# Three edits of order and place in a pair of linear-attention blocks: PSUM banks of the second block's kv products, SBUF places of the raw x^T, order of the first transfers

## The chip, the cores and the metric

The kernel runs on one core of a Trainium2 chip. Time is device microseconds (us) of one execution. The kernel before takes 582.83 us (median of 3 runs, 582.18 to 585.84). Lower is better.

## The reference

Two independent blocks, A and B, have the same form; their outputs stand side by side in the last axis. With S = 2048 tokens, D = 640, H = 32 heads of 20:

```
qkv = x @ wqkv                       # q, k, v: [H, S, 20]
pq, pk = phi(q), phi(k)              # phi(t) = where(t > 0, t + 1, exp(t)) + 1e-6
kv  = einsum("hsd,hse->hde", pk, v)
z   = sum over s of pk
o   = (pq @ kv) / (pq . z + 1e-6)
out = o (heads joined) @ wo          # [S, 640] per block
```

## The kernel before

**What is computed in which form.** Every fp32 product that needs accuracy is made of three TensorE products: each operand is split into a high part (ScalarE, a copy that rounds) and a low part (VectorE, the raw value minus the high part), and high times high, high times low and low times high are summed in PSUM. kv is not formed from v: the kernel first sums G = x^T phi(k) over all tokens ("gacc", five row blocks of 128), then kv = wv^T G by groups of heads, masks it to its diagonal blocks, and multiplies it by wo. So after the k stage of a block there is one matrix M = kv wo (640 x 640) with which phi(q), divided, is multiplied. Products with wk and with M are in part done by a seven-product scheme on half blocks, with sums of operands made on VectorE.

**Two ways of setting order.** The k stage of both blocks is written as jobs (`note`, line 86) that a planner (`emit`, line 113) puts in order by due times with a model of each engine; TensorE's own order is that in which the jobs were written. A job's due time is worked back from those that need its result; among the jobs that can start, the one due first goes first. The same planner gives raw data their SBUF places: `BD` (line 256) has 7 places of 640 columns with the tag "wst", `BO` 4 and `GD` 31. The q stage behind it (from line 863 on) is written out by hand: `at(slot, f, ...)` hangs a step on a slot such as ("q", u, c, k), and `run` does what hangs there when the TensorE instructions of that slot have been written. u counts blocks of 512 tokens (u = 0 to 3 are block A's, 4 to 7 block B's), c the five column blocks of q, k the five parts of the contraction.

**The first transfers.** x^T of the first three token tiles ("xj", five row blocks) and wk (five row blocks, the first in two halves) come first: `load_joint` (line 626), the two halves at line 633 and `load` (line 286). xj's block 0 is issued by ScalarE's queue, all others by SyncE's (SP). TensorE has seven short products on a zero tile ("idle", line 614) ahead of the first real ones (`one`, line 661).

**The q stage's banks.** `bank` (line 865) hands out the eight PSUM banks in four rings (line 862): "one" is banks 0 to 2, "a" 3 and 4, "e" 5 and 6, "small" 7. `qmm` (line 1036) takes a bank of ring "one" for each of the five q products of a token block, 15 matmuls each; `qphi` then reads that bank twice on ScalarE (lines 1056 and 1057: exp and relu). In the first token block (u = 0), block B's kv products are put in between: `kvmm2` (line 941), for each of six groups of heads, two per q product in c = 0, 1, 2 (at k = 0 and k = 3). It also takes its bank ("pskv") from ring "one"; VectorE reads it once (line 952, the mask). `mmm2` (line 962) multiplies by wo in a bank of "a" and one of "e".

**The q stage's SBUF places.** Block B's wv, cut in six groups, is loaded by the planner into six of the seven "wst" places, group by group, and each is freed by the last matmul of its `kvmm2`. In the same slots the raw x^T of token block 1 ("xqs", five parts, `load_xraw`, line 916) is loaded into "wst" places too: `stage` (line 902) and `turned` (line 870) go round the seven places, 0 to 6. In the kernel before the planner has put group 0 of wv in place 0, group 5 in place 1, groups 1, 2, 3 and 4 in places 2, 3, 4 and 5; place 6 is free. Behind these loads SP's queue has, in written order, the first parts of block A's M forms ("fh", "fl", `form_load`, line 1018) and the low parts of x^T ("xql", `load_xq`, line 921). The low parts have six places: five hold token block 0's, so only the first of token block 1's can be loaded early, and each of the other four waits until TensorE has read one of block 0's for the last time, in ("q", 0, 4, k).

**Transfers in flight.** SP's transfers count on eight semaphores in turn ("DMAHW0" to "DMAHW7"): each waits until the one eight before it has landed. SP issues in order, so a transfer that waits holds up all behind it.

Of the kernel before, what the change touches and what calls it, by code (L numbers as in the profile page):

```python
# [75 lines left out]
class Plan:  # L76
# [6 lines left out]
        self.jobs = []  # L83
        self.pe_at = 0.0

    def note(self, engine, n, fn, w, r, ahead=None, dma=None, late=None, by=None):
        base = self.RATE.get(engine)
        j = Job(engine, base[0] + base[1] * n if base else n, fn, ahead, dma)
        for part, writes in [(p, True) for p in w] + [(p, False) for p in r]:
            sp = part.space  # L90
            if sp.where is not None and sp not in j.spaces:
                j.spaces.append(sp)
            for lo, hi, other, wrote in sp.uses:
                if lo < part.hi and part.lo < hi and (writes or wrote) and other is not j:
                    j.deps.add(other)
            if writes:
                sp.uses = [u for u in sp.uses if not (part.lo <= u[0] and u[1] <= part.hi and u[2] is not j)]
            sp.uses.append((part.lo, part.hi, j, writes))
        for d in j.deps:
            d.nexts.append(j)  # L100
        for sp in j.spaces:
            sp.left += 1
        if engine == "PE":
            j.ideal = self.pe_at
            self.pe_at += j.cost
        j.late = self.pe_at + (25.0 if late is None else late)
        if by is not None:
            j.late = self.pe_at + by
        j.by = by
        self.jobs.append(j)  # L110
        return j

    def emit(self, start, log=None):
        jobs = self.jobs
        for j in reversed(jobs):
            due = min([n.due - LAG for n in j.nexts], default=j.late)
            if j.by is not None:
                due = min(due, j.late)
            due -= j.cost + (2.2 + j.dma if j.dma else 0)
            if j.engine == "PE":  # L120
                due = min(due, j.ideal)
            j.due = due

        def take(sp):
            for s in sp.where:
# [10 lines left out]
        n = 0  # L136
# [67 lines left out]
def tile_linear_attn_pair(ctx: ExitStack, tc: tile.TileContext, ins, out: bass.AP):  # L204
    nc = tc.nc
    P = 128
    S, D = ins[0]["x"].shape
# [3 lines left out]
    HF = D // 2  # L211
# [54 lines left out]
    note = plan.note  # L266
# [16 lines left out]

    BK = [Bank("bank", k) for k in range(8)]

    def load(dst, src, n, ahead=14.0, eng=None):
        eng = eng or nc.sync
        note("SP", 0.07, lambda: eng.dma_start(dst.f, src), [dst], [], ahead=ahead, dma=n * 512 / 330e3)

    def hi_of(hi, src, n):  # L290
        note("ACT", n, lambda: act(hi.r, src.f, AF.Copy), [hi], [src], ahead=10.0)
# [332 lines left out]
    jr, wr = [Space("xj", 3 * P, ANY) for _ in range(NC)], [Space("wk", D, ANY) for _ in range(NC)]  # L624

    def load_joint(c, eng):
        src = ins[0]["xt"][c * P:(c + 1) * P, 0:3 * P]
        note("SP", 0.07, lambda: eng.dma_start(jr[c].all.f, src), [jr[c].all], [], dma=0.6)

    load_joint(0, nc.scalar)  # L630
    for h in range(2):
        cs = slice(h * HF, (h + 1) * HF)
        note("SP", 0.07, lambda h=h, cs=cs: nc.sync.dma_start(wr[0][h * HF:h * HF + HF].f, ins[0]["wk"][:P, cs]),
             [wr[0][h * HF:h * HF + HF]], [], dma=0.5)
    for c in range(1, NC):
        load_joint(c, nc.sync)
        load(wr[c].all, ins[0]["wk"][c * P:(c + 1) * P, :], D, None)

    def whalf(h, *t):
        return [x[0][h * HF:h * HF + HF] for x in t]  # L640
# [124 lines left out]
    for p in range(4, NPB):  # L765
        i, h = divmod(p - 2, 2)
# [9 lines left out]
    for p in range(NPB + 2, NP):  # L776
        i, h = divmod(p - NPB - 2, 2)
# [17 lines left out]
    j = note("HOST", 0.0, swap, [gate.all], [])  # L795
# [9 lines left out]
    wst, whl, wvt, xt, xts = {}, {}, {}, {}, {}  # L805
# [41 lines left out]
    for g, (h0, nh) in enumerate(GROUPS):  # L847
        cols = NC * DH * nh
        w = Space("wv", cols, (BD,))
# [5 lines left out]
        whl[k] = hi.tile, lo.tile  # L855
    for k, (hi, lo) in list(xt.items()):
        xt[k] = [hi.tile, lo.tile]
    for k, w in list(wvt.items()):
        wvt[k] = w.all.f.rearrange("p (c e) -> p c e", c=NC)
    close_pool(kg, "kg")  # L860
# [2 lines left out]
    pn, turn = {}, {}  # L863

    def bank(name, tag="one", bufs=3):
        at, n = ptags[tag]
        pn[tag] = pn.get(tag, -1) + 1
        return psum.tile([P, 512], F32, name=name, tag=f"bank{at + pn[tag] % n}", bufs=1)

    def turned(tag, n):  # L870
        turn[tag] = (turn.get(tag, -1) + 1) % n
        return f"{tag}{turn[tag]}"

    lows = []

# [26 lines left out]
    def stage(name):  # L902
        return base.tile([P, D], F32, name=name, tag=turned("wst", 7), bufs=1)
# [37 lines left out]
    def kvmm2(b, g):  # L941
        h0, nh = GROUPS[g]
        r = DH * nh
        w = wvt.pop((b, g))
        ps = bank("pskv")
        for c in range(NC):
            gd = gacc[b, c].rearrange("p (d h) -> p d h", h=H)[:, :, h0:h0 + nh]
            nc.tensor.matmul(ps[:r, :r].rearrange("p (d h) -> p d h", h=nh), w[:, c, :], gd,  # L948
                             start=(c == 0), stop=(c == NC - 1))
        t = base.tile([r, r], F32, name="kvt", tag="kvt0", bufs=1)  # L950
        hi, lo = (base.tile([r, r], F32R, name=f"kv{t}", tag=turned("kvs", 12), bufs=1) for t in "hl")
        nc.vector.tensor_tensor(t, ps[:r, :r], mask[nh][:r, :], op=OP.mult)
        split(hi, lo, t)
        kvt[b, g] = (hi, lo)
# [299 lines left out]
    h = NG - 1  # L1254
# [24 lines left out]
    for v in range(1, NU):  # L1279
        w, u = v - 1, v + 1  # L1280
# [86 lines left out]
```

## Time and profile before

| | |
|---|---|
| median of 3 runs | 582.83 us (582.18 to 585.84) |
| the profiled execution's own time | 583.46 us |
| its span in the profile | 581.6 us |
| TensorE busy | 568.3 us, 98% of the span |
| VectorE, ScalarE busy | 431.0 us (74%), 341.8 us (59%) |
| granted TensorE clock, mean | 0.996 |

The span is shared out between engines in the profile's first part. The timeline gives each instruction's start, its length and, in brackets, how long its engine had been idle before it and what ended that. The waits list adds up those times by pair of instructions. A name such as `psq<-xqh,wh` is the output and the operands by the program's names. "SPq" rows are the issue of a transfer, not the transfer. The windows view gives, for a stretch of time, each engine's busy time with the count of instructions in brackets, the granted clock ("PEclk"), and the share of time that the transfer engines were busy.

### The profile page before, as it was taken

What the parts mean: (1) busy time and instruction counts of PE and PEld (TensorE: products, weight loads), DVE (VectorE), ACT (ScalarE), POOL (GpSimd) and SP (SyncE); (2) the same over time, 40 slices, a digit from 0 to 9 for tenths busy, and PEclk for the clock granted to TensorE, in tenths of its full rate; (3) what the DMA queues carried; (4) which work ended last, traced back from release to release, by engine and by line L of the source; (5) the groups of instructions that cost most, each with busy time, mean ns of one, the idle gap of its engine ahead of it and who ended that gap; (6) DMA issues with size and microseconds to landing.
All of it is one profiled execution on the core that took longest, in us unless ns stands there. A gap on an engine that the chain in (4) does not pass through costs nothing.

```text
span 581.6 us, 9507 instructions
## 1 busy us (share of the span) xinstructions
PE 568.3 (98%) x3541; PEld 537.7 (92%) x3541; DVE 431.0 (74%) x700; ACT 341.8 (59%) x619; POOL 57.3 (10%) x93
## 2 busy tenths in 40 slices
PE   8999999999999999999989799999999999999997
PEld 6999999999998999999967689898998989898897
DVE  7688687689777878874444498967789775757792
ACT  6878465573769766763435565744647455545541
POOL 0210011110011011111000001211011200001010
PEclk9999999999999999999999899999999999999999
DMA  8994847748768898778745975674183897122022
GB/s 311 368 249 121 218 115 191 195 115 265 240 160 254 280 279 250 202 211 249 238 109 190 391 263 171 223 248 157 63 278 109 310 393 258 70 74 92 0 91 90
DMA packets 67857, 117.60 MB, mean 202 GB/s; under 512 B 6500, under 2 KB 29668, under 8 KB 67812
## 3 DMA queue, kind: packets, MB, share of 16 engines
q1 hardware_dynamic: 59060, 89.94, 47.3%
q0 software_dynamic: 8608, 26.88, 16.7%
q8 instruction: 27, 0.44, 0.3%
q10 hardware_dynamic: 144, 0.20, 0.1%
q14 instruction: 18, 0.15, 0.1%
HBM read 71.11 MB, written 35.39 MB: 183 GB/s over the span
## 4 chain that ended last, share of the span: by engine, by line
PE 89%; DMA 5%; issue 2%; ACT 2%; DVE 1%; SPq 0%; ACTq 0%; DVEq 0%; POOLq 0%
PE psg L300 23%; PE pa L1167 12%; PE ka L300 8%; PE psq L888 8%; PE psq L889 8%; PE psq L890 7%; PE pe L1167 6%; PE ke L300 4%; PE psk L689 4%; PE psb L1167 4%; PE kb L300 3%; DMA zacc<-ek 2%; DMA xql<-xd 1%; DMA xqs<-in_A_xt 1%; PE pskv L948 1%
## 5 line engine op out<-in xcount | busy, mean ns | idle before, releaser
L300 PE MATMUL psg<-pkh,xnh 128*128 128x320 f32 x320 | 99.1, 310 | 0.0
L300 PE MATMUL psg<-pkl,xnh 128*128 128x320 f32 x320 | 98.8, 309 | 0.0
L300 PE MATMUL psg<-pkh,xnl 128*128 128x320 f32 x320 | 98.7, 308 | 0.0
L888 PE MATMUL psq<-xqh,wh 128*128 128x512 f32 x200 | 79.4, 397 | 3.7 <-ACT rq L1057 3.7
L889 PE MATMUL psq<-xql,wh 128*128 128x512 f32 x200 | 78.7, 394 | 3.1 <-DMA xql<-xd 3.1
L890 PE MATMUL psq<-xqh,wl 128*128 128x512 f32 x200 | 78.6, 393 | 0.0
L300 PEld LDWEIGHTS psg<-pkh,xnh 128*128 128x128 f32 x320 | 60.0, 188 | 0.1
L300 PEld LDWEIGHTS psg<-pkl,xnh 128*128 128x128 f32 x320 | 60.1, 188 | 0.0
L300 PEld LDWEIGHTS psg<-pkh,xnl 128*128 128x128 f32 x320 | 60.1, 188 | 0.0
L1182 ACT ACTIVATE o<-pa 128x320 f32<-128x320 f32 x64 | 28.0, 438 | 47.1 <-PE pa L1167 46.9
L1058 DVE SCALAR_TENSOR_TENSOR pq<-eq,rq 128x512 f32<-128x512 f32 x40 | 27.6, 690 | 35.5 <-ACT rq L1057 35.5
L471 ACT ACTIVATE kt<-ka 128x320 f32<-128x320 f32 x52 | 22.7, 437 | 52.9 <-PE ka L300 52.3
L388 POOL DMA_DIRECT2D zacc<-ek x32 | 26.4, 836 | 244.5 <-DVE ek L481 186.7
L519 DVE TENSOR_TENSOR gacc<-psg,gacc 128x320 f32<-128x320 f32 x60 | 29.1, 489 | 28.1 <-PE psg L300 27.3
L888 PEld LDWEIGHTS psq<-xqh,wh 128*128 128x128 f32 x200 | 37.8, 189 | 12.2 <-ACT rq L1057 5.0
L889 PEld LDWEIGHTS psq<-xql,wh 128*128 128x128 f32 x200 | 38.0, 190 | 10.8 <-DMA xql<-xd 3.5
L1056 ACT ACTIVATE eq<-psq 128x512 f32<-128x512 f32 x40 | 24.0, 599 | 40.6 <-PE psq L890 38.2
L890 PEld LDWEIGHTS psq<-xqh,wl 128*128 128x128 f32 x200 | 38.0, 190 | 8.1
L383 ACT ACTIVATE pkh<-ek,epst 128x640 fp32r<-128x640 f32 x32 | 26.5, 829 | 8.5 <-DVE ek L481 8.4
L1167 PE MATMUL pa<-fh,dah 128*128 128x320 f32 x96 | 29.7, 309 | 0.0
L1167 PE MATMUL pa<-fl,dah 128*128 128x320 f32 x96 | 29.6, 309 | 0.0
L1167 PE MATMUL pa<-fh,dal 128*128 128x320 f32 x96 | 29.6, 308 | 0.0
(212 smaller groups left out, 1551.7 us busy)
## 6 DMA issues: line engine op xcount, KB each, us to landing
zacc<-ek POOLq DMA_DIRECT2D x32, 320.0 KB, 5.0
xql<-xd SPq DMA_DIRECT2D x40, 256.0 KB, 5.3
xd<-xl SPq DMA_DIRECT2D x29, 320.0 KB, 4.5
out<-o POOLq DMA_DIRECT2D x28, 320.0 KB, 3.6
xns<-in_A_x SPq DMA_DIRECT2D x16, 320.0 KB, 4.2
xts<-in_B_xt_tiles SPq DMA_DIRECT2D x16, 320.0 KB, 4.2
xns<-in_B_x SPq DMA_DIRECT2D x16, 320.0 KB, 6.8
xqs<-in_A_xt SPq DMA_DIRECT2D x20, 256.0 KB, 4.8
```

Of the source, the lines that this page charges most:

```text
L300: nc.tensor.matmul(o, a.r, w.r, start=start and k == i == 0, stop=k == n - 1 and i == 2, skip_group_check=True)
L383: note("ACT", n + 110, lambda: act(hi.r, p.f, AF.Identity, bias=epst), [hi], [p, K0.all], by=8.0)
L388: note("POOL", 1.0, lambda: nc.gpsimd.dma_start(z.f, p.f, **kw), [z], [p], dma=1.0 if first else 1.86)
L519: tt(o, BK[k].tile[:, :HF], o, op=OP.add)
L689: nc.tensor.matmul(o[h][:, :HF], x[a].r, w[c][h * HF:h * HF + HF].r, start=c == 0 and i == 0, stop=c == NC - 1 and i == 2, skip_group_chec ...
L888: nc.tensor.matmul(o, whi, xhi, start=first, stop=False)
L889: nc.tensor.matmul(o, whi, xlo, start=False, stop=False)
L890: nc.tensor.matmul(o, wlo, xhi, start=False, stop=last)
L1056: nc.scalar.activation(e, ps, AF.Exp)
L1058: nc.vector.scalar_tensor_tensor(pq[u][:, c, :], e, 1.0, r, op0=OP.min, op1=OP.add)
L1167: nc.tensor.matmul(ps, x, y, start=start and n == i == 0, stop=n == len(terms) - 1 and i == 2, skip_group_check=True)
L1182: copy = lambda x, y: nc.scalar.activation(x, y, AF.Copy)
```

## The change

It has three parts.

- `kvmm2` takes its bank from ring "e" (banks 5 and 6) in place of ring "one" (banks 0 to 2).
- The ring of "wst" places starts with those that hold no group of wv, and then goes through the groups' places in the order of the groups. In the changed kernel the planner puts group 0 in place 6 and leaves place 0 free; the others stand as before. The ring is then 0, 6, 2, 3, 4, 5, 1, so the five parts of xqs of token block 1 go to the free place and to the places of groups 0, 1, 2 and 3. Before, they went to places 0, 1, 2, 3, 4: those of groups 0, 5, 1, 2 and 3.
- The first transfers have due times that are set by hand: wk's first half, xj's block 0, wk's second half, and then xj and wk of block 1, 2, 3, 4 in turn.

```diff
-    def note(self, engine, n, fn, w, r, ahead=None, dma=None, late=None, by=None):
+    def note(self, engine, n, fn, w, r, ahead=None, dma=None, late=None, by=None, due=None):
...
-        j.by = by
+        j.by, j.set = by, due
...
-            j.due = due
+            j.due = due if j.set is None else j.set
...
-    def load(dst, src, n, ahead=14.0, eng=None):
-        eng = eng or nc.sync
-        note("SP", 0.07, lambda: eng.dma_start(dst.f, src), [dst], [], ahead=ahead, dma=n * 512 / 330e3)
+    def load(dst, src, n, ahead=14.0, due=None):
+        note("SP", 0.07, lambda: nc.sync.dma_start(dst.f, src), [dst], [], ahead=ahead, dma=n * 512 / 330e3, due=due)
...
-        note("SP", 0.07, lambda: eng.dma_start(jr[c].all.f, src), [jr[c].all], [], dma=0.6)
-
-    load_joint(0, nc.scalar)
+        note("SP", 0.07, lambda: eng.dma_start(jr[c].all.f, src), [jr[c].all], [], dma=0.6, due=-99.0 + 2 * c)
     for h in range(2):
         cs = slice(h * HF, (h + 1) * HF)
         note("SP", 0.07, lambda h=h, cs=cs: nc.sync.dma_start(wr[0][h * HF:h * HF + HF].f, ins[0]["wk"][:P, cs]),
-             [wr[0][h * HF:h * HF + HF]], [], dma=0.5)
+             [wr[0][h * HF:h * HF + HF]], [], dma=0.5, due=-100.0 + 2 * h)
+    load_joint(0, nc.scalar)
     for c in range(1, NC):
         load_joint(c, nc.sync)
-        load(wr[c].all, ins[0]["wk"][c * P:(c + 1) * P, :], D, None)
+        load(wr[c].all, ins[0]["wk"][c * P:(c + 1) * P, :], D, None, -98.0 + 2 * c)
...
+    places = [w.slot[1] for w in wvt.values()]
+    places = [i for i in range(7) if i not in places] + places
...
-        return f"{tag}{turn[tag]}"
+        return f"{tag}{places[turn[tag]] if tag == 'wst' else turn[tag]}"
...
-        ps = bank("pskv")
+        ps = bank("pskv", "e", 2)
```

TensorE's instructions stand in the same order in both kernels; what differs there are waits. The first place is TensorE at the switch from block B's second kv group to the end of the first q product (u = 0, c = 0, k = 4) and on to c = 1: `psq` is a q product's bank, `pskv` a kv product's, and the brackets name the engines or transfers whose semaphores an instruction waits for. Before:

```order
L948 MATMUL pskv<-gacc,wv 120x120 [waits DMAHW0_49]
L948 MATMUL pskv<-gacc,wv 120x120 x4
L888 MATMUL psq<-xqh,wh 128x512 [waits Activation_49]
L889 MATMUL psq<-xql,wh 128x512 [waits DMAHW7_49]
L890 MATMUL psq<-xqh,wl 128x512 [waits DVE_49]
L888 MATMUL psq<-xqh,wh 128x512 [waits Activation_49]
L889 MATMUL psq<-xql,wh 128x512
```

Now:

```order
L948 MATMUL pskv<-gacc,wv 120x120 [waits DMAHW0_49,PE_49]
L948 MATMUL pskv<-gacc,wv 120x120 x4
L888 MATMUL psq<-xqh,wh 128x512 [waits Activation_49]
L889 MATMUL psq<-xql,wh 128x512 [waits DMAHW7_49]
L890 MATMUL psq<-xqh,wl 128x512 [waits DVE_49]
L888 MATMUL psq<-xqh,wh 128x512
L889 MATMUL psq<-xql,wh 128x512
```

The wait for ScalarE (Activation) at the first matmul of the q product c = 1 is gone, and so it is at c = 2 and c = 3; the kv product of group 1 now follows TensorE's own earlier use of its bank.

The second place is SP in the same stretch: the five raw parts of x^T (xqs), the first three pairs of M forms (fh, fl) and the first low parts (xql) of token block 1. The order of the transfers is the same; the waits differ. Before:

```order
L919 DMA xqs<-in_A_xt 128x512 [waits DMAHW2_49,PE_49]
L919 DMA xqs<-in_A_xt 128x512 [waits DMAHW3_49,PE_49]
L919 DMA xqs<-in_A_xt 128x512 [waits DMAHW4_49]
L919 DMA xqs<-in_A_xt 128x512 [waits DMAHW5_49]
L1032 DMA fh<-fdh_90 128x640 [waits DMAHW6_49]
L1032 DMA fl<-fdl_91 128x640 [waits DMAHW7_49]
L919 DMA xqs<-in_A_xt 128x512 [waits DMAHW0_49]
L1032 DMA fh<-fdh_92 128x640 [waits DMAHW1_49]
L1032 DMA fl<-fdl_93 128x640 [waits DMAHW2_49]
L1032 DMA fh<-fdh_94 128x640 [waits DMAHW3_49]
L1032 DMA fl<-fdl_95 128x640 [waits DMAHW4_49]
L923 DMA xql<-xd_81 128x512 [waits DMAHW5_49]
```

Now:

```order
L919 DMA xqs<-in_A_xt 128x512 [waits DMAHW2_49]
L919 DMA xqs<-in_A_xt 128x512 [waits DMAHW3_49,PE_49]
L919 DMA xqs<-in_A_xt 128x512 [waits DMAHW4_49,PE_49]
L919 DMA xqs<-in_A_xt 128x512 [waits DMAHW5_49,PE_49]
L1032 DMA fh<-fdh_90 128x640 [waits DMAHW6_49]
L1032 DMA fl<-fdl_91 128x640 [waits DMAHW7_49]
L919 DMA xqs<-in_A_xt 128x512 [waits DMAHW0_49,PE_49]
L1032 DMA fh<-fdh_92 128x640 [waits DMAHW1_49]
L1032 DMA fl<-fdl_93 128x640 [waits DMAHW2_49]
L1032 DMA fh<-fdh_94 128x640 [waits DMAHW3_49]
L1032 DMA fl<-fdl_95 128x640 [waits DMAHW4_49]
L923 DMA xql<-xd_81 128x512 [waits DMAHW5_49]
```

Before, the second xqs waited for TensorE's kv product of group 5, the last, and the third, fourth and fifth had nothing left to wait for there. Now each waits for one group in turn: none, 0, 1, 2, 3.

The third place is the start on VectorE, where the high and low parts of the first xj and wk are made (ScalarE makes the other high parts in the same new order: wk's first half ahead of xj's columns 128 to 383). Before:

```order
L648 CAST xjh<-xj 128x128
L294 TENSOR_TENSOR xjl<-xj,xjh 128x128
L294 TENSOR_TENSOR xjl<-xj,xjh 128x256
L294 TENSOR_TENSOR wkl<-wk,wkh 128x320
L294 TENSOR_TENSOR wkl<-wk,wkh 128x640
L294 TENSOR_TENSOR wkl<-wk,wkh 128x320
```

Now:

```order
L646 CAST xjh<-xj 128x128
L293 TENSOR_TENSOR xjl<-xj,xjh 128x128
L293 TENSOR_TENSOR wkl<-wk,wkh 128x320
L293 TENSOR_TENSOR xjl<-xj,xjh 128x256
L293 TENSOR_TENSOR wkl<-wk,wkh 128x320
L293 TENSOR_TENSOR xjl<-xj,xjh 128x384
```

wk's first half now goes ahead of xj's 256 columns, and wk's second half ahead of wk's block 1. Because the planner goes on from another state, some neighbours on ScalarE and VectorE change places later in the k stage too, above all while block A's kv and wo parts are made.

## The prediction

> **What bounds the kernel now.** I read the page's engine shares first, then the list of waits for TensorE (PE), then the timeline around each wait, then SP's timeline.
>
> ```profile
> PE 568.3 (98%) x3541; PEld 537.7 (92%) x3541; DVE 431.0 (74%) x700; ACT 341.8 (59%) x619; POOL 57.3 (10%) x93
> ...
> PE psq L888 <- ACT rq L1057: 3.7, 3, 1.2
> PE psq L889 <- DMA xql<-xd: 3.1, 1, 3.1
> PE psk L666 <- ACT wkh L291: 1.6, 1, 1.6
> ...
> PE ka L300 <- ACT kt L471: 0.5, 2, 0.3
> ...
> 32.00:290.00 258.00, 257.33 (x1777) 256.12 (x1776) 198.09 (x363) 165.83 (x293) 23.43 (x28) 1.00 0.75 212
> ...
> 345.00:566.00 221.00, 221.00 (x1251) 202.29 (x1250) 172.41 (x231) 119.76 (x218) 25.97 (x48) 1.00 0.49 172
> ```
>
> TensorE is busy in all but 13.3 of 581.6 us, so only its own stops can be won back. The list (total, times, longest) names 9.9 us of them: three of 1.2 us and one of 3.1 us in the q products (psq), the rest at the start or small. The two windows (length, then busy time of PE) show that from 32 to 290 us and from 345 to 566 us there is next to nothing to win: 0.67 and 0.00 us. What the change can be worth lies between 290 and 345 us, and at the start.
>
> **The three short stops: banks.** TensorE and ScalarE at the first of them:
>
> ```profile
> 295.99 0.40 PE L890 MATMUL psq<-xqh,wl 128*128 128x512 f32 x1
> 297.62 0.50 PE L888 MATMUL psq<-xqh,wh 128*128 128x512 f32 x1 [1.23 <-ACT rq L1057]
> 297.95 0.39 PE L889 MATMUL psq<-xql,wh 128*128 128x512 f32 x1
> 298.18 0.39 PE L890 MATMUL psq<-xqh,wl 128*128 128x512 f32 x1
> ...
> 296.48 0.60 ACT L1056 ACTIVATE eq<-psq 128x512 f32<-128x512 f32 x1
> 296.98 0.59 ACT L1057 ACTIVATE rq<-psq 128x512 f32<-128x512 f32 x1
> ```
>
> Between the q products of c = 0 and c = 1 stand two kv products. With three banks in ring "one" (q, kv, kv, q) the next q product comes back to the bank that the last one has only just filled, and ScalarE reads it twice, until 297.57. The matmul starts at 297.62. With kv out of that ring the q products go 0, 1, 2, and each finds a bank that was read long ago: the order of the changed kernel has no wait for ScalarE at that matmul.
>
> What a stop costs is more than its idle time, since the first matmul behind it is slower. From 295.99 to 297.95 are two steps; undisturbed a step is 0.23 (297.95 to 298.18), so 1.96 - 0.46 = 1.50 us. Three of them: 4.5 us.
>
> What the kv products meet in ring "e": they alternate between banks 5 and 6, with one bank for each `mmm2` among them. The closest pair in one bank are the kv products of groups 4 and 5:
>
> ```profile
> 305.49 0.88 PE L948 MATMUL pskv<-gacc,wv 128*80 128x80 f32 x10
> 306.40 0.24 DVE L952 TENSOR_TENSOR kvt<-pskv,mask 80x80 f32<-80x80 f32 x1 [0.25 <-PE pskv L948]
> ...
> 309.20 0.88 PE L948 MATMUL pskv<-gacc,wv 128*80 128x80 f32 x10
> ```
>
> VectorE has read group 4's bank at 306.64, 2.6 us ahead of group 5's start. Bounds: 0, or, if each kv had to wait out a read as q does now, all 4.5 us back. I take 0; the order adds only a wait for TensorE's own earlier write and for VectorE's last adds into gacc, which the first kv product needs anyway.
>
> **The long stop: places.**
>
> ```profile
> 295.47 0.37 SPq L919 DMA_DIRECT2D xqs<-in_A_xt  x1
> 310.11 1.61 SPq L919 DMA_DIRECT2D xqs<-in_A_xt  x3
> ...
> 311.04 5.67 DMA xqs<-in_A_xt
> 316.73 8.39 DMA xql<-xd
> ...
> 321.66 0.39 PE L888 MATMUL psq<-xqh,wh 128*128 128x512 f32 x1
> 325.16 0.79 PE L889 MATMUL psq<-xql,wh 128*128 128x512 f32 x1 [3.11 <-DMA xql<-xd]
> 328.29 0.39 PE L890 MATMUL psq<-xqh,wl 128*128 128x512 f32 x1
> ...
> 325.16:328.29 3.13, 3.13 (x8) 2.48 (x9) 2.33 (x4) 1.88 (x3) 0.00 (x0) 0.51 1.04 391
> 297.62:298.41 0.79, 0.79 (x3) 0.66 (x4) 0.67 (x1) 0.08 (x1) 0.00 (x0) 1.00 1.04 226
> ```
>
> SP issues one xqs at 295.47 and then nothing until 310.11: the second goes to the place of kv group 5, whose product ends at 309.20 + 0.88 = 310.08. All that is behind it starts together from there. The fourth xqs, issued at 311.04, lands at 316.71, and the first xql, eight transfers on, can be issued only then; it lands at 325.12, and TensorE, which wanted it from 321.89, starts at 325.16. After that stop the granted clock is 0.51 for 3.13 us. From 321.66 to 328.29 are eight steps that take 1.84 us undisturbed, so the stop costs 6.63 - 1.84 = 4.8 us.
>
> In the changed order the waits are for groups 0, 1, 2 and 3. The last of these:
>
> ```profile
> 301.55 1.21 PE L948 MATMUL pskv<-gacc,wv 128*120 128x120 f32 x10
> 316.72 0.39 PE L889 MATMUL psq<-xql,wh 128*128 128x512 f32 x1
> ...
> DMA to landing us min/median/max: 7.1/7.6/8.2
> ...
> xql<-xd SPq DMA_DIRECT2D x4, 256.0 KB, 3.7
> ...
> 296.00:311.00 15.00, 12.35 (x78) 9.88 (x76) 6.16 (x15) 6.66 (x15) 0.68 (x1) 1.00 0.29 69
> 311.00:325.00 14.00, 10.00 (x49) 8.43 (x49) 5.50 (x8) 9.54 (x19) 1.84 (x3) 0.99 0.98 338
> ```
>
> Group 3 ends at 302.76, less the one stop ahead of it (1.5) at 301.3. The fifth xqs goes out then, six M forms behind it at some 0.5 us each, and the first xql at about 305, where TensorE wants it at 321.89 - 4.5 = 317.4. Even with 8.4 us it is there by 314. So the wait on the first xql goes.
>
> **What is late next** are the second to fifth xql. Each waits until TensorE has read a part of token block 0: the first such read ends at 316.72 + 0.39 = 317.11. Its part is wanted one k step and one matmul behind 321.66 (0.69 + 0.23), at 322.58: there is room for 5.5 us, whatever else shifts. The trace has two answers for how long such a copy takes from issue to landing: 7.1 to 8.2 us in this burst, and 3.7 us for the four copies issued between 344 and 350 us. In this burst the transfer engines are 0.98 busy (last but one column of the window); from 296 to 311 they are 0.29 busy, and it is there that the change puts the xqs and the first six M forms, 5 x 256 + 6 x 320 KB, about 8 us at the 391 GB/s of the row above. When the second xql is issued, at 312.6, these are through, so I take 3.7 to 5.5 and a stop of 0; the other end is 7.6 - 5.5 = 2.1 us.
>
> A stop of 2.1 us would, by the rows above, lie between 1.23 idle, which kept the clock at 1.00, and 3.11, which brought 0.51; I keep 2.1 to 3.7 (with another 1.6 for the slow clock) as its price. [...]
>
> **The chain behind u = 0.** The long stop hid one thing: the sum for the divisors of token block 0 (denmm).
>
> ```profile
> 325.33 0.63 ACT L882 ACTIVATE ac<-acc 128x512 fp32r<-128x512 f32 x1 [1.55 <-DVE acc L1068]
> 326.00 0.69 DVE L879 TENSOR_TENSOR ac<-acc,ac 128x512 fp32r<-128x512 f32 x1 [0.70 <-ACT ac L882]
> ```
>
> These follow TensorE's work before 321.66, so they shift with it. Measured from 321.66 they are ready at 4.3 and 5.03; undisturbed, denmm's two matmuls come seven k steps on, at 4.8 and 5.03. That is just in time: 0 to 0.3 us, I take 0.1.
>
> **The start.**
>
> ```profile
> 4.86 0.42 ACT L291 ACTIVATE xjh<-xj 128x256 fp32r<-128x256 f32 x1 [2.40 <-DMA xj<-in_A_xt]
> 5.18 0.45 ACT L291 ACTIVATE wkh<-wk 128x320 fp32r<-128x320 f32 x1
> ...
> 5.12 0.63 DVE L294 TENSOR_TENSOR xjl<-xj,xjh 128x128 fp32r<-128x128 f32 x2
> 5.67 0.49 DVE L294 TENSOR_TENSOR wkl<-wk,wkh 128x320 fp32r<-128x320 f32 x1
> 5.69 3.00 PE psk L666 x18
> ...
> 5.69 0.42 PE L666 MATMUL psk<-wkh,xjh 128*128 128x320 f32 x1 [1.56 <-ACT wkh L291]
> 6.24 0.31 PE L666 MATMUL psk<-wkh,xjl 128*128 128x320 f32 x1
> ```
>
> TensorE starts at 5.69, when ScalarE has made wkh, which stands behind xjh. Now wkh goes first, so the first matmul can start up to 0.5 us earlier. But the fourth matmul (6.24) needs the low part of xj's 256 columns, and on VectorE that now stands behind wkl. If wk's half has landed by 4.86: wkh to 5.3, wkl to 5.8, the low part (0.63 less the 128-column one, some 0.4) to 6.2, and the fourth matmul starts where it did. If it landed only at 5.18, the same chain ends near 6.55, 0.3 later. So -0.1 to +0.3; I take 0. The transfers moved behind (wk's block 1, from second to fourth) have cover: that block is wanted only behind the 18 matmuls of block 0, which take 3.00 us, and the list of waits has no other psk stop. Without cover each would cost its lateness, below 1 us. [...]
>
> The later swaps on ScalarE and VectorE while block A's kv and wo are made cost nothing as long as TensorE has work ahead, as it has there; without that, about 0.3 for each bank copy that comes late (the ka row), in some three places: up to 1.
>
> **The sum**, against the profiled execution (583.46: a span of 581.6 and 1.9 around it): -4.5 - 4.8 + 0.1 + 0 = -9.2, a span of 572.4 and 574.3 in all. That execution is 0.6 above the median of the runs, so for the median 582.83 - 9.2 = **573.6 us**, 1.6% less.
>
> **The rivals.**
>
> *The next xql are late* (0.15). For it: the room is 5.5 us and the burst's copies took 7.1 to 8.2. Against it: those shared the engines with all that SP had held back. 2.1 to 3.7 back: 575.7 to 577.3.
>
> *One of the two edits does not bring its part* (0.08): the kv products or `mmm2` wait in ring "e" as q did, or SP is held elsewhere, say by the wo loads just ahead of xqs. 4.5 or 4.8 back: 578.1 to 578.4. Against it are the waits in the new order.
>
> *Slower: the clock* (0.03). TensorE is then busy 99% without the pauses; if a denser stream lowered the granted clock over the whole program, each percent would cost 5.7 us. From a mean of 0.984 the gain is eaten; at 0.97 the time would be 591. Against it: 221 us without any idle time, at 1.00.
>
> **How the numbers follow.** The forecast has 0.74. The range of 572.4 to 577.4 goes from the forecast with the start's gain, no denmm stop and some spread of the runs (their lowest is 0.65 under their median) to the full price of the late xql. A difference under 1%, 5.8 us, is about what a measurement of this kernel cannot tell from no change. Faster by more than that (below 577.0) are the forecast and most of the first rival: 0.87. Within 1%: the second rival and the dear end of the first: 0.10. Slower: 0.03.
>
> **What would show it.** Right: no psq stop on ScalarE's rq; SP's xqs issued from 295 to 302 one by one; the xql wait gone, and the clock 1.00 from 290 to 345; the first `outmm` matmul near 336.8, where it was at 345.99. Wrong: a wait of psq on xql at k = 1 to 4 (first rival), pskv or psm with idle time ahead (second), or a PEclk below 1.00 where TensorE is fully busy (third). A first matmul before 5.3 with the fourth still near 6.24 would show the start as I put it.

## The result and the profile after

The changed kernel takes 575.63 us (median of 4 runs, 575.38 to 576.41) beside 583.03 us for the kernel before: a ratio of 0.987, 95% interval 0.983 to 0.990. That is 2.0 us above the forecast of 573.6 and within its range. The profiled execution took 575.42 us with a span of 573.5 us, 8.1 less than before. One run of the kernel before, in the series of e5 to e8, took 1923.41 us; it counts in no ratio.

The page's engine shares, the list of waits for TensorE, and four windows (length, busy time of PE, PEld, DVE, ACT and POOL, granted clock, DMA share, GB/s):

```profile
PE 567.6 (99%) x3541; PEld 538.5 (94%) x3541; DVE 430.7 (75%) x700; ACT 340.3 (59%) x619; POOL 57.3 (10%) x93
```

```profile
PE psk L664 <- DVE xjl L293: 1.0, 1, 1.0
PE psi L617 <- DVE ones L307: 1.0, 1, 1.0
PE ka L299 <- ACT kt L470: 0.5, 1, 0.5
```

```profile
0.00:32.00 32.00, 29.99 (x178) 27.62 (x179) 23.20 (x48) 22.69 (x45) 4.17 (x11) 1.00 0.96 321
32.00:290.00 258.00, 257.34 (x1776) 256.23 (x1775) 198.14 (x362) 164.95 (x292) 23.43 (x28) 1.00 0.76 214
290.00:336.00 46.00, 46.00 (x256) 39.62 (x256) 29.95 (x49) 28.04 (x55) 3.70 (x6) 1.00 0.84 267
336.00:557.00 221.00, 221.00 (x1248) 202.04 (x1247) 173.81 (x232) 120.21 (x218) 25.96 (x48) 1.00 0.49 173
```

The list has no wait of the q products (psq) any more; from 290 to 336 us TensorE is busy in all of 46.00 us, at a clock of 1.00. What is left idle lies in the first 32 us. The k stage and the outputs have not changed: 257.34 of 258 us busy, and 221 of 221.

TensorE where the first of the three short stops was: the kv products of group 0, then the q product c = 1.

```profile
295.49 1.21 PE L948 MATMUL pskv<-gacc,wv 128*120 128x120 f32 x10
296.46 0.48 PE L888 MATMUL psq<-xqh,wh 128*128 128x512 f32 x1
296.78 0.39 PE L889 MATMUL psq<-xql,wh 128*128 128x512 f32 x1
```

The q product follows the kv products at once, with no wait for ScalarE's rq. SP in the same stretch, and the xql of this stretch from issue to landing:

```profile
295.55 3.95 SPq L919 DMA_DIRECT2D xqs<-in_A_xt  x4
299.56 0.42 SPq L1032 DMA_DIRECT2D fh<-fdh  x1
...
302.31 0.33 SPq L919 DMA_DIRECT2D xqs<-in_A_xt  x1
302.69 0.43 SPq L1032 DMA_DIRECT2D fh<-fdh  x1
...
304.60 11.42 SPq L923 DMA_DIRECT2D xql<-xd  x5
316.07 0.45 SPq L1032 DMA_DIRECT2D fh<-fdh  x1
```

```profile
DMA to landing us min/median/max: 4.1/4.1/4.1
```

Four xqs go out between 295.55 and 299.5, the fifth at 302.31, and the first xql at 304.60 (forecast: 295 to 302, and about 305). Each xql lands 4.1 us after its issue; there was room for 5.5.

The divisors' sum (denmm, psd), which the long stop had hidden:

```profile
322.53 0.69 DVE L879 TENSOR_TENSOR ac<-acc,ac 128x512 fp32r<-128x512 f32 x1 [0.70 <-ACT ac L882]
...
323.00 0.39 PE L1078 MATMUL psd<-ac,same 128*128 128x512 f32 x1
323.28 0.50 PE L1079 MATMUL psd<-ac,same 128*128 128x512 f32 x1
323.61 0.40 PE L888 MATMUL psq<-xqh,wh 128*128 128x512 f32 x1
```

VectorE is done at 323.22, and the second psd starts at 323.28. The two together take 323.61 - 323.00 = 0.61 us where two undisturbed steps take 0.46: a stop of 0.15.

The start:

```profile
4.53 0.23 DVE L646 CAST xjh<-xj 128x128 fp32r<-128x128 f32 x1 [1.81 <-DMA xj<-in_A_xt]
...
4.66 0.47 ACT L290 ACTIVATE wkh<-wk 128x320 fp32r<-128x320 f32 x1 [2.21 <-DMA wk<-in_A_wk]
...
5.18 0.64 PE L664 MATMUL psk<-wkh,xjh 128*128 128x320 f32 x1 [1.02 <-DVE xjl L293]
5.62 0.47 PE L664 MATMUL psk<-wkh,xjl 128*128 128x320 f32 x1
5.88 0.47 PE L664 MATMUL psk<-wkh,xjh 128*128 128x320 f32 x1
6.15 0.53 PE L664 MATMUL psk<-wkh,xjl 128*128 128x320 f32 x1
...
9.48 0.31 PE L664 MATMUL psk<-wkl,xjh 128*128 128x320 f32 x1
9.63 0.46 PE L687 MATMUL psk<-wkh,xjh 128*128 128x320 f32 x2
```

The first matmul starts 0.51 earlier than before (5.18 for 5.69). It reads wkh and xjh, and what let it start earlier is wkh: ScalarE makes it from 4.66 to 5.13, as soon as wk's first half has landed, where before it began at 5.18, behind xjh. (The bracket names xjl, which VectorE finished at about the same time.) But from start to start a step takes 0.267 us (5.62 to 5.88 to 6.15), where before it took 0.147, and that goes on for some 14 matmuls. The 18 matmuls of wk's block 0 take 4.45 us (5.18 to 9.63) for 2.84 before (5.69 to 8.53), and what follows is 1.1 us late.

To see where the rest went, I took the start of each TensorE instruction less its start in the kernel before. At the first matmul it is -0.51, at block 1 of wk (L687) +1.10, at the beginning of the q stage (289.55 before) +1.00, after each of the three former short stops -0.47, -1.97 and -3.47, behind denmm -8.14, and about -8.0 at the end. So the stretch from 290 to 336 us gave 9.14 us, and the start took back 1.1.

### The profile page after: what moved, and what is told of

Its sections match the earlier page's. It is cut to its first block, busy times and chain, and to the rows that moved or that the text cites. A ratio compares the mean times of both kernels' runs of the same rounds, so it can differ in the third digit from the quotient of the medians.

```text
span 573.5 us, 9515 instructions
## 1 busy us (share of the span) xinstructions
PE 567.6 (99%) x3541; PEld 538.5 (94%) x3541; DVE 430.7 (75%) x700; ACT 340.3 (59%) x619; POOL 57.3 (10%) x93
## 4 chain that ended last, share of the span: by engine, by line
PE 97%; ACT 1%; DMA 1%; DVE 0%; issue 0%; DVEq 0%
PE psg L299 24%; PE pa L1167 12%; PE ka L299 10%; PE psq L888 8%; PE psq L890 8%; PE psq L889 8%; PE pe L1167 6%; PE ke L299 5%; PE psk L687 4%; PE psb L1167 4%; PE kb L299 3%; PE pskv L948 1%; PE pskv L537 1%; PE psm L564 1%; PE psk L664 1%; DMA xj<-in_A_xt 1%
```

## The experiments

Two questions were open: whether the two edits of the q stage are worth what the sum says, each alone and together; and whether the half pace of the first matmuls comes from the new order of the first transfers, or from something that differs between executions of the same code.

All measurements in one table. Each row's ratio is to the kernel before on the same chip. "18 matmuls" is the time from the first psk matmul to the first of wk's block 1 in that kernel's profile; "Clock rises at" is where the trace's own record of TensorE's granted clock begins, in us from the start of the span: its first entry is full speed, and ahead of it there is none. "q stage" is what the stretch from 289.55 to 331.75 us changed against the kernel before, worked out as above.

| kernel | median us (range, runs) | ratio (95%) | first psk at | 18 matmuls | clock rises at | q stage |
|---|---|---|---|---|---|---|
| before | 583.03 (582.18-585.84, 4) | | 5.69 | 2.84 | 3.96 | |
| changed | 575.63 (575.38-576.41, 4) | 0.987 (0.983-0.990) | 5.18 | 4.45 | 8.89 | -9.14 |
| e1_banks | 581.97 (580.84-582.63, 10) | 0.9975 (0.9958-0.9992) | 6.08 | 2.85 | 4.81 | -3.70 |
| e2_places | 580.48 (579.19-581.60, 6) | 0.9944 (0.9924-0.9963) | 5.61 | 2.84 | 4.09 | -4.66 |
| e3_start | 581.79 (578.95-584.73, 9) | 0.9964 (0.9944-0.9985) | 4.58 | 3.35 | 3.82 | -2.85 |
| e4_banks_places | 574.38 (574.11-577.08, 6) | 0.9848 (0.9826-0.9870) | 5.60 | 4.66 | 9.89 | -9.15 |
| e6_after_again | 574.61 (572.94-575.95, 6) | 0.9847 (0.9822-0.9872) | 5.37 | 4.70 | 9.65 | -9.13 |
| e7_b_p_again | 576.22 (575.21-577.22, 6) | 0.9881 (0.9859-0.9904) | 5.97 | 4.10 | 9.00 | -9.13 |
| e5_idle9 | 573.74 (573.46-574.13, 4) | 0.9840 (0.9814-0.9865) | 5.04 | 3.76 | 6.94 | -9.17 |
| e8_idle1 | 575.04 (574.29-575.84, 4) | 0.9862 (0.9835-0.9888) | 4.85 | 4.86 | 9.27 | -9.16 |
| e11_idle12 | 574.60 (574.33-575.10, 4) | 0.9838 (0.9811-0.9864) | 5.73 | 3.87 | 5.91 | -9.13 |
| e9_cols | 576.12 (1 run) | | 5.91 | 2.88 | 4.21 | -9.15 |
| e10_rows | 577.21 (1 run) | | 6.54 | 4.42 | 4.01, half again from 7.43 to 10.84 | -9.17 |
| e12_forms_late | 583.37 (582.15-585.43, 10) | 0.9990 (0.9975-1.0005) | 5.11 | 4.43 | 8.59 | -0.85 |

### The banks alone

The kernel before, with this one line:

```
-        ps = bank("pskv")
+        ps = bank("pskv", "e", 2)
```

> The kernel before with the kv banks alone changed. My theory: the three stops on rq go (4.5 us), but the place edit is missing, so SP still waits for kv group 5. That product has two stops ahead of it, not three, so it and the chain of 15 us behind it move forward by only 3.0 us while TensorE wants the low part 4.5 us earlier: the long stop grows by 1.5 us to some 4.6 idle, the gain is 3.0 us, 580.0 us. Rival (the two edits are independent): 4.5 us, 578.5 us, the long stop as before at 3.1.

The first of the waits for TensorE, and the window behind the long stop:

```profile
PE psq L889 <- DMA xql<-xd: 4.0, 1, 4.0
```

```profile
322.76:326.02 3.26, 3.26 (x8) 2.64 (x9) 2.12 (x3) 1.16 (x2) 0.00 (x0) 0.55 1.03 399
```

The three stops on rq are gone and are worth 4.49 us up to the q product with the long stop. Of these the long stop takes back 0.79: its xql comes 2.4 us earlier than before (the matmul that waits starts at 322.76 instead of 325.16), since the kv products that free its way end earlier, but TensorE gets there sooner still and waits 4.0 us instead of 3.1; the clock behind the stop is again about half, 0.55. The two edits are therefore not independent, and the banks alone are worth 3.70 us in this profile, between the two expectations.

### The places alone

The kernel before, with the ring of places in the order in which kv frees them:

```
+    places = [w.slot[1] for w in wvt.values()]
+    places = [i for i in range(7) if i not in places] + places
...
-        return f"{tag}{turn[tag]}"
+        return f"{tag}{places[turn[tag]] if tag == 'wst' else turn[tag]}"
```

> The kernel before with the ring of places alone changed. My theory: the three stops on rq stay (3.7 us idle), the wait on xql and the slow clock behind it go: 4.8 us, 578.2 us. Rival (the low parts two to five are late, as their transfers are issued only when TensorE has read a part): a stop of up to 2.1 us stays, 580.3 us.

The first of the waits for TensorE:

```profile
PE psq L890 <- ACT rq L1059: 3.7, 3, 1.2
```

The three short stops stay as they were and no wait on xql is in the list. The edit is worth 4.66 us in this profile: the forecast's 4.8 less denmm's stop.

In medians the two edits are worth less than in the profiles: 1.5 us for the banks alone and 3.0 for the places alone (583.50 for the kernel before in this series), beside 9.1 for both (e4). Part of a reason stands in the mean granted clock of the single runs. One stretch of 3.41 us at half clock, as in the profile of the kernel before (324.82 to 328.23 us, at 0.50), takes 0.003 off a mean over 582 us (an estimate: half of 3.41 in 582). The kernel before has 0.997 in 10 of the 18 runs of this series and 0.999 or 1.000 in 8, the banks alone 0.994 to 0.997 in all ten, the places alone 1.000 in all six. So it seems that only about half of the runs of the kernel before pay for a half clock behind the long stop, as its profile does, and that all ten with the banks alone do. Where in those runs the clock fell is not recorded, and the rest of the difference stays open.

### The order of the first transfers alone

The kernel before, with the order of the first transfers set (wk's first half, its second half, xj's block 1, wk's block 1, and so on) and nothing else:

```
-    def note(self, engine, n, fn, w, r, ahead=None, dma=None, late=None, by=None):
+    def note(self, engine, n, fn, w, r, ahead=None, dma=None, late=None, by=None, due=None):
...
-            j.due = due
+            j.due = due if j.set is None else j.set
```

with the `due=` values at the loads as in the change.

> The kernel before with the order of the first transfers alone changed. Theory A (the new order causes the slow first matmuls: start at 5.2 us, then 0.27 us a step for 3.5 us): first k step (L687) at 9.6 in place of 8.5, 584.1 us. Theory B (the slow steps come from where the clock's change happens to fall in that execution, whatever the order): first matmul at 5.2, and a pace of 0.147 or 0.27 by chance; with the fast pace the fourth matmul near 6.0 and the first k step at 8.2 to 8.4, 582.8 us.

The waits and TensorE's first matmuls:

```profile
PE psq L886 <- ACT rq L1055: 3.7, 3, 1.2
PE psq L887 <- DMA xql<-xd: 1.6, 1, 1.6
```

```profile
4.58 0.39 PE L664 MATMUL psk<-wkh,xjh 128*128 128x320 f32 x1 [0.53 <-DVE xjh L646]
...
5.63 0.41 PE L664 MATMUL psk<-wkh,xjl 128*128 128x320 f32 x1 [0.18 <-DVE xjl L293]
...
7.78 0.31 PE L664 MATMUL psk<-wkl,xjh 128*128 128x320 f32 x1
7.93 0.46 PE L687 MATMUL psk<-wkh,xjh 128*128 128x320 f32 x2
```

With the new order TensorE starts at 4.58 and, once the operands are there, goes at 0.147 us a step: block 1 begins at 7.93, 0.6 earlier than before. So the new order does not by itself bring the half pace. At the fourth matmul it does wait for xj's low part behind wkl, as the forecast's chain has it, only that all of it stands 0.6 earlier. The gain of 2.85 in the q stage does not come from the edit, which changes nothing there: in this execution the long stop had 1.6 us and no lower clock behind it, where the profile of before shows 3.1 us and 0.51. One execution's long stop is not another's. In medians e3 is 1.7 us faster than the kernel before of its series (ratio 0.9964), and 8 of its 9 runs have a mean clock of 0.999 or 1.000; whether the edit or chance spared them the half clock is not shown.

### Banks and places without the order of the first transfers

The changed kernel with its third edit undone; e4 is that kernel, and e7 the same kernel again in another series, beside e6, the changed kernel unaltered.

> The changed kernel with the first transfers as they were before. Theory A (the order causes the slow first matmuls): first matmul at 5.7 at a pace of 0.147, no stop from 290 to 336, 573.8 us, 1.1 us below the changed kernel's profile. Theory B (chance): slow first matmuls as often as in the changed kernel; the median within 0.5 us of the changed kernel's 575.6.

> The changed kernel once more, unaltered, beside the other three. If the slow first matmuls are chance of the execution (theory B), this profile may show a pace of 0.147 from the start, with the first k step at 7.9 to 8.4, or 0.27 with it at 9.6; from 290 to 336 us no stop in either case. If the new order causes them (theory A), 0.27 again. Median 575.0, as between the earlier 575.6 and the 574.4 of the version without the start edit.

> Banks and places without the start edit, once more. If the order of the first transfers is worth what the profiles show at equal pace (0.6 us), this is 0.6 above the unaltered changed kernel of this call: 575.6. Rival, from the two medians so far (574.4 against 575.6): 1.2 below it.

The start of e4:

```profile
5.60 0.64 PE L666 MATMUL psk<-wkh,xjh 128*128 128x320 f32 x1 [1.43 <-ACT wkh L291]
6.03 0.47 PE L666 MATMUL psk<-wkh,xjl 128*128 128x320 f32 x1
6.30 0.47 PE L666 MATMUL psk<-wkh,xjh 128*128 128x320 f32 x1
...
10.26 0.45 PE L689 MATMUL psk<-wkh,xjh 128*128 128x320 f32 x2
```

Here the old order goes at half pace too (6.03 to 6.30), and the clock's record begins only at 9.89. The order as the cause of the half pace falls: old and new order each show both paces, and in every profile the pace goes with the clock's record ("clock rises at" in the table). The q stage gives 9.15 and 9.13 without the third edit and 9.13 with it.

What the third edit is worth cannot be told from the medians: without it the kernel was 1.2 us faster than the changed one, measured apart from it (574.38 and 575.63), and 1.6 slower beside it in one series (576.22 and 574.61). In profiles at one pace it is some 0.5 us, from one to three profiles each: at the full pace block 1 began at 7.93 with it and at 8.45, 8.53 and 8.93 without; at half pace at 9.54 (e12), 9.63 and 10.07 with it, 10.07 and 10.26 without.

### More and fewer idle matmuls ahead of the first real one

Before its first operands land, the kernel lets TensorE run seven matmuls whose result is not used. The changed kernel with one, nine and twelve:

```
-        for i in range(7):
+        for i in range(9):
```

> The changed kernel with one idle matmul in place of seven. Theory (the clock): the pace is 0.27 in every execution from the first real matmul on for 3.4 us or more, the first k step at 9.6 or later, 0.5 to 1.6 us above the changed kernel on the median. Rival (slow steps from the transfers): no change.

> The changed kernel with nine idle matmuls ahead of the first real ones in place of seven, so that TensorE has work until 5.0 us. [...] Rival (the slow first steps come from operands read while the first transfers are written): slow as often as with seven, the median unchanged.

> The changed kernel with twelve idle matmuls in place of seven. They take TensorE to 6.3 us if the clock does not rise under them, and less if it does; the first real matmul is then at 5.6 to 6.3 and the pace 0.147 soon after. The first k step at 8.5 to 9.2, so about what nine gave (8.80): 573.7. Rival (more idle work only delays): 1.2 us above nine, 574.9.

With one idle matmul the clock's record begins at 9.27 us, 4.42 behind the first real matmul at 4.85, with seven at 8.89 (the changed kernel), with nine at 6.94 and with twelve at 5.91; block 1 begins at 9.71, 9.63, 8.80 and 9.60. So twelve had the full pace earliest, and still block 1 was later than expected. VectorE's low part of xj, and the matmul that waits for it:

```profile
6.21 0.29 DVE L293 TENSOR_TENSOR xjl<-xj,xjh 128x128 fp32r<-128x128 f32 x1 [0.96 <-PE psi L617]
...
7.29 0.41 PE L664 MATMUL psk<-wkh,xjl 128*128 128x320 f32 x1 [0.17 <-DVE xjl L293]
```

The profile names the idle matmuls (psi), which end at 6.17 here, as what VectorE waits for ahead of xjl: 0.96 us with twelve, 0.16 with nine. The second and the fourth real matmul then wait for low parts (0.24 and 0.17 us). So in these two profiles the clock came up sooner than in the changed kernel's (6.94 and 5.91 for 8.89), but the operands were held up.

They are one execution each, though, and the same code spreads by as much (2.84 and 4.66 us for the 18 matmuls in the old order with seven). In medians, one against seven in the same series is +0.4 us with overlapping ranges, not to be told apart; nine is 0.9 below seven, and its four runs lie within 0.7 us. It has the lowest median of the study, 573.74 us, ratio 0.984 (0.981 to 0.987); twelve, in another series, is level with it by its ratio to the kernel before of that series (0.9838). The lead of nine over the changed kernel is within the spread of the latter's runs (572.94 to 576.41), so it isn't shown to be a gain.

### When xj lands

The first matmul needs xj's block 0, which ScalarE's queue issues at 0.7 us in all kernels. In twelve of the profiles its cast (xjh) starts on landing: at 4.77 to 5.25 in the five profiles with the old order (before, e1, e2, e4, e7), and with the new at 4.21 to 4.75 in six (changed, e3, e5, e6, e8, e12) and at 5.03 in one (e11). To see whether what SP issues beside it decides this, wk's block 1 was cut in two halves and put back between wk's first halves, in two column halves and in two row halves:

```
+        if c == 1:
+            for h in range(2):
+                cs = slice(h * HF, (h + 1) * HF)
+                note("SP", 0.07, lambda h=h, cs=cs: nc.sync.dma_start(wr[1][h * HF:h * HF + HF].f, ins[0]["wk"][P:2 * P, cs]),
+                     [wr[1][h * HF:h * HF + HF]], [], dma=0.5, due=-99.5 + 2 * h)
+            continue
```

The row halves have in place of the fourth of these lines:

```
+                note("SP", 0.07, lambda h=h: nc.sync.dma_start(wr[1].all.f[h * 64:h * 64 + 64], ins[0]["wk"][P + h * 64:P + h * 64 + 64, :]),
```

> The changed kernel with wk's block 1 loaded in two halves of columns (rows of 1280 bytes), the first half as SP's second transfer and the second as its fourth. The first xj landed at 4.77 to 5.25 us in five profiles of the old order, where SP's second transfer is 320 KB in rows of 2560 bytes, and at 4.21 to 4.75 in five of the new, where it is 160 KB in rows of 1280. Theory R (the length of the rows that go in turn with xj's decides): 4.2 to 4.75 here. Theory S (the size of the second transfer decides): 4.2 to 4.75 too.

> The same with wk's block 1 loaded in two halves of partitions (64 rows of 2560 bytes each), in the same places of SP's order and with the same 160 KB. Theory R (length of the rows): the first xj lands late, at 4.77 to 5.25 us. Theory S (size of the second transfer): 4.2 to 4.75.

VectorE in e9:

```profile
5.14 0.49 DVE L293 TENSOR_TENSOR wkl<-wk,wkh 128x320 fp32r<-128x320 f32 x1 [2.42 <-ACT wkh L290]
5.55 0.22 DVE L652 CAST xjh<-xj 128x128 fp32r<-128x128 f32 x1
```

xj was cast at 5.55 and at 6.18, but that is not when it landed: with these two edits the planner has put wkl ahead of the cast on VectorE, and the cast follows it without idle time. The landing is read from the trace's packets instead. ScalarE's queue carries this one transfer (144 packets, 0.20 MB); its last packet ends at 4.07 us in e9 and at 4.15 in e10. In the other profiles it ends at 4.40 to 4.87 with the old order and at 3.75 to 4.55 with the new, 0.30 to 0.49 us ahead of the cast. By that distance xj was there at some 4.4 to 4.6 us in both (an estimate), early as theory S has it; the length of the rows (theory R), by which e10 should have been late, is not borne out. These are one profile each, and one with the new order (e11, 4.55) lies among those with the old, so what SP's first transfers do to xj is suggested and not shown.

The first matmul began at 5.91 and 6.54. e9 went at full pace (2.88 us for the 18); e10 began at full pace, fell to half at 7.43 and took 4.42.

### The M forms behind the second xql

The forecast's first rival was that other transfers on the way make the xql late. The changed kernel has three pairs of M forms (fh, fl) ahead of the first xql, in the quiet stretch before 304 us. This one issues them behind the second:

```
-        at((("q", 0, 2, 1), ("q", 0, 2, 4), ("q", 0, 3, 1), ("q", 1, 0, 0), ("q", 1, 0, 2), ("q", 1, 1, 0))[i],
+        at((("q", 0, 4, 1), ("q", 0, 4, 1), ("q", 0, 4, 1), ("q", 1, 0, 0), ("q", 1, 0, 2), ("q", 1, 1, 0))[i],
```

> The changed kernel with the first six M forms issued behind the second low part of x^T of token block 1 in place of ahead of the fifth raw part, so that they are on the way when the third to fifth low parts are. My account of the place edit (what counts is that the transfers SP had held back are through by then): the low parts take 6 to 8 us again, a stop on xql of 1 to 3 us comes back, 1 to 4 us above the changed kernel. Rival (the edit's worth is only the earlier first low part): no stop, no change.

SP, TensorE at the q product that waits, the xql's time from issue to landing, and a window behind the stop:

```profile
313.18 0.33 SPq L923 DMA_DIRECT2D xql<-xd  x1
313.56 0.45 SPq L1032 DMA_DIRECT2D fh<-fdh  x1
...
316.87 2.15 SPq L923 DMA_DIRECT2D xql<-xd  x3
```

```profile
326.15 0.80 PE L889 MATMUL psq<-xql,wh 128*128 128x512 f32 x1 [6.66 <-DMA xql<-xd]
```

```profile
DMA to landing us min/median/max: 2.6/5.1/9.2
```

```profile
326.10:329.50 3.40, 3.35 (x8) 2.68 (x9) 0.00 (x0) 0.00 (x0) 0.00 (x0) 0.51 1.04 407
```

Six transfers of 320 KB stand between the second and the third xql; at the window's 407 GB/s they alone are 4.8 us of work for the transfer engines (an estimate). The third xql, issued at 316.87, lands 9.2 us later at 326.1, TensorE has waited 6.66 us, and 3.4 us at a clock of 0.51 follow. The whole gain is gone: 583.37 us beside 584.26 for the kernel before. The mechanism of the rival is right, and its price is 8.3 us (-0.85 for -9.14) where 1 to 4 were expected: 6.66 of idle time and about 1.7 at the lower clock (an estimate: half of 3.4).

## Why the prediction was right, and what it missed

**The three bank stops, 4.5 us:** right. Each former stop moves TensorE by 1.5 us (-0.47, -1.97, -3.47), and ring "e" takes nothing back: neither pskv nor psm has a wait. In e1 the three give 4.49.

**The long stop, 4.8 us:** right in mechanism and size: 4.66 in e2, with denmm's stop in it. SP's issues, the 305 for the first xql, and the clock of 1.00 stand as forecast. But 4.8 is the cost in one execution; e3 shows 1.6 us of idle time with no lower clock behind it, and of the 41 runs of the kernel before that stand beside the experiments 22 have a mean clock of 0.997, as one stretch of half clock would give (the profiled execution has 0.996), and 19 have 0.999 or 1.000. That the two terms add up is so only with the low parts in time: in e1 the long stop grew by 0.79.

**The second to fifth xql, 0:** right. 4.1 us from issue to landing for 5.5 of room. e12 shows how much hung on it: the quiet stretch from 296 to 304 us is where the M forms have to go.

**denmm, 0.1:** 0.15 us, within its bounds.

**The swaps at no cost:** right. wk's block 1, issued fourth, has no wait, and the k stage is busy for 257.34 us where it was 257.33. But from block 1 to the q stage the profiles differ from the kernel before by -1.2 (e8) to +0.8 us (e1), whatever the edit; the changed kernel's has -0.1. The forecast had no term for that.

**The sum of the q stage, -9.2:** -9.14, and between -9.13 and -9.17 in all nine profiles that have both edits and the M forms where the change has them.

**The start, 0 with bounds of -0.1 and +0.3:** this is the term that was wrong, at +1.1 us in the profile. Both signs that the forecast named for it came (a first matmul before 5.3, at 5.18; the fourth near 6.24, at 6.15), yet not by its reasoning, and the fourth is luck: it did not wait for the low part of xj, which VectorE had done by 5.99, it was late because the first three went at half pace. In place of the term the runs showed two things. wkh, made first, brought the first matmul forward by 0.51, the forecast's "up to 0.5"; that xj landed earlier too (the cast at 4.53 for 4.86) was not needed for it, since from 4.86 its cast of 0.23 us would have been done by 5.09, ahead of wkh at 5.13. And the clock rose only at 8.89 us, so that some 14 matmuls went at 0.267 us a step: +1.6 over the 18. The 0.147 of the profile before was taken as what this stretch costs, although there the clock had happened to rise at 3.96, and e4 and e7 show the same order at half pace.

How this gives 2.0 us: the profiled execution changed by 8.04 us (583.46 to 575.42) instead of 9.2. Of these 1.16 us the start is 1.1; -0.1 between block 1 and the q stage, 0.06 that the q stage fell short of 9.2 and 0.09 behind it make up the rest. The other 0.84 is where the profiled executions lie among the runs: before's stood 0.63 above its median, and the forecast took off the full 9.2 from the median; after's stands 0.21 below its own. In the second series the changed kernel had 574.61, 1.0 above the forecast. The first matmul of the outputs, for which the forecast named 336.8, came at 337.67 (345.83 before), late by what the start had lost.

**The rivals.** That one edit brings nothing is refuted by e1 and e2, a clock lowered by a denser stream by the mean of 1.000. The late xql did not come about, and is real (e12).

## What to carry to other kernels

A ring's order decides which stop a buffer makes: give a place to the one who frees it first, and look at what its wait holds up in the same queue, here 14.6 us in which SP issued nothing. Two stops in a row on one engine need not add up: here removing the first alone lengthened the second (3.1 to 4.0 us of idle time in e1), so undo each alone and both together. The 18 matmuls at the start took from 2.84 to 4.66 us in five profiles with one order of transfers, so such a stretch is not priced from one profile; look at it in several executions first, and give its term the width that they show.

## What was not expected of the hardware

**The half pace at the start does not show in the clock column of the changed kernel's profile.** The window over the changed kernel's slow matmuls:

```profile
5.60:8.75 3.15, 3.15 (x13) 3.06 (x13) 2.08 (x5) 2.41 (x5) 0.00 (x0) 1.00 0.98 341
```

The clock column has 1.00 where steps take 0.267 us for 0.147; behind the stop in e12 it has 0.51 where they take 0.43 for 0.23, about the same ratio. The trace's clock records say why: they begin with the first rise, at 8.89 us in this profile, and where there is none the view counts full speed. In all 14 profiles the pace follows these records ("clock rises at" in the table). e10 has both a rise ahead of its first real matmul and a fall behind it, and there the column shows the half clock:

```profile
4.01:7.43 3.42, 1.03 (x6) 0.80 (x6) 1.62 (x5) 1.25 (x3) 0.00 (x0) 1.00 1.03 253
7.43:10.84 3.41, 3.41 (x15) 3.41 (x14) 2.54 (x5) 2.67 (x5) 0.00 (x0) 0.50 1.00 344
```

**The changes of the clock lie whole multiples of 3.41 us apart in these traces, and at other times in each execution.** In the kernel before the records change at 3.96, 324.82, 328.23 and 580.82 us: 94 times, once and 74 times that from one to the next. In the changed kernel it is 166 times (8.89 to 575.50), in e10 once from 4.01 to 7.43 and once more to 10.84. The same code rose at 8.89 and at 9.65 us in two executions (changed and e6). In the 14 profiles the first rise went with how much of the 3.41 us ahead of it TensorE was busy. Here are those 3.41 us in e1 and, in the changed kernel, a stretch at whose end the clock did not rise, 3.41 us ahead of the rise:

```profile
1.40:4.81 3.41, 2.76 (x7) 0.73 (x5) 1.23 (x6) 1.06 (x1) 0.40 (x2) 1.00 0.80 209
2.07:5.48 3.41, 2.39 (x6) 0.76 (x5) 1.46 (x6) 1.20 (x4) 0.00 (x0) 1.00 0.95 289
```

2.76 of 3.41 us is 81%, the smallest share ahead of a first rise; the largest in an earlier stretch of 3.41 us, at whose end the clock did not rise, is 74% (0.12 to 3.53 in e5). The clock fell behind 30% in e10, above, and behind 19% in the kernel before (0.65 of 3.42 us, 321.40 to 324.82). It did not fall behind 54% in the kernel before (1.86 of 3.42 us, 3.96 to 7.38), nor behind 45% in the changed one (1.55 of 3.41, 568.68 to 572.09). The seven idle matmuls are 3.17 us of work (0.99 to 4.16 in the changed kernel). With seven the clock rose at 3.82 to 4.81 us in six profiles, whose last 3.41 us before the rise were busy for 81 to 93%. In the other five it rose at 8.59 to 9.89, behind 89 to 100%, and had not risen 3.41 us earlier, behind 58 to 72%. What sets these changes is not shown beyond that.

A stop of 3.11 us in the kernel before and one of 2.39 in e10 each brought the half clock for 3.41 us. A stretch of 3.41 us that held a stop of 2.1 us whole would be busy for 38% (an estimate), between the 30% and the 45% above, so what the forecast's stop of 2.1 us would have cost is not shown.

**How long an xql took differed by more than twice with what was queued beside it:** 4.1 us in the changed kernel, up to 8.2 in the burst of before, 9.2 behind six transfers of 320 KB (e12).

**xj's landing at the start** went with the order of the transfers on another queue: its last packet ended at a median of 4.18 us with the new order (seven profiles) and 4.49 with the old (five). In e9 and e10, with wk's block 1 in halves, it ended at 4.07 and 4.15. What decides it is left open.
